# The second layer's row blocks run last to first, under one nested test, in a fused attention and two-MoE kernel

## The chip, the cores and the metric

One NeuronCore of a Trainium2 chip runs the whole program. The metric is the device time of one execution in microseconds; the times of the kernel before are 552.27, 552.94 and 557.62 us, median 552.94 us.

## What is computed

Chunked attention (2 x 8 heads, 768 tokens, head size 64, with 8 memory tokens) gives 1536 rows of 512. Two mixture-of-experts layers with 8 experts follow, each token going to its best expert. The reference, cut to the expert work of the second layer:

```python
expert_idx = np.argmax(logits, axis=1)          # logits = x @ w_gate
for i in range(N):                              # N = 1536, capacity = 384
    e = expert_idx[i]
    if counts[e] < capacity:
        disp[e, counts[e]] = x[i]; pos[i] = counts[e]; counts[e] += 1; keep[i] = True
h = np.maximum(np.einsum('ecd,edf->ecf', disp, w1), 0.0)   # D = 512, F = 1024
y = np.einsum('ecf,efd->ecd', h, w2)
out[i] = gate_w[i] * y[expert_idx[i], pos[i]]              # for kept tokens
```

## The kernel before, in words

The program is attention (to about 85 us), the routing of layer 0, eight experts of layer 0, the routing of layer 1 (about 313 to 329 us), and eight experts of layer 1. An order written out by hand holds on every engine: each engine runs its instructions in the order in which the code issues them.

A matmul in full precision is made of three: each fp32 operand is split into a rounded high part and a low remainder, and high x high, high x low and low x high are added up in one PSUM bank. So every weight half (w1 or w2 of one expert, 2 MB) is cut into 8 pieces; a piece costs a cast on ACT (L756, `whi`) and a subtraction on DVE or POOL (L757, `wlo`). The raw halves come by SP's DMAs into a ring of three slots, so a slot is loaded again only when all its pieces were cast and subtracted.

One expert of layer 1 (`layer_run`, layer 1) goes through these steps:

- `gather(e + 1)` and `scatter(e - 1)` are issued on POOL (indirect DMAs of the rows that go to the expert, and of its results).
- `first(e)`: h = relu(x w1) in eight products of 12 matmuls (L818 to L820), each in the next of four PSUM banks; their width is 224, 320 or 384 columns, chosen by up to two tests on the expert's number of tokens (`by_width`, the branches carry L775). ACT and DVE take each product into `hx` (L834, L835) and, between them, split the pieces of w2.
- `columns(e + 1)`: 12 transposes (L803) turn the next expert's rows into columns, into two of the four banks and one further; ACT (L807) and DVE (L808) copy them out.
- `second_rows(e)`: y = h w2, in blocks of 128 tokens. A block is 24 matmuls (L878 to L880) into one bank. Block 0 always runs; blocks 1 and 2 each stand under a `tc.If` on the token count (L885), so an expert runs one, two or three blocks. Between the blocks, the pieces of the next expert's w1 are split (3, 3 and 2 of them), and `rows` (L894) scales a finished block's bank into `yr` on ACT. The last expert already takes its blocks as 2, 1, 0, and scatters each as soon as it is scaled.

A `tc.If` on PE is: two register operations and a compare-and-branch, the body, a branch over the other arm, and in the other arm a wait on PE's own semaphore and a raise of it by what the body would have raised, so that waits of other engines count the same on both ways. The profile shows that wait as an EVENT_SEMAPHORE of PE's sequencer (PEq, L885).

Layer 0 uses `second_columns` in place of `second_rows` and is not touched.

Of the kernel before, what the change touches and what calls it, by code (L numbers as in the profile page):

```python
# [32 lines left out]
def kernel(  # L33
# [15 lines left out]
    nc = tc.nc  # L49
    B, _, _, D, _ = q.shape  # L50
    H, S = 2 * q.shape[1], SEQ
    N, DM = out.shape
    E, _, F = w1a.shape
    P = 128
# [6 lines left out]
    KF = F // P  # L61
# [3 lines left out]
    NA = CAP // P  # L65
    NAF = N // P
    XW = DM + E
    STEP = 32
# [14 lines left out]
    hx = [wpool.tile([P, KF, CAP], F32, name=f"hx{z}") for z in range(2)]  # L83
# [111 lines left out]
    def fr(ap):  # L195
        return ap.bitcast(F32R)
# [549 lines left out]
    def pieces(i, j, pool=(), done=0):  # L746

        if i < 2 * E:
            for n in range(PIECES):
                yield parts(i, j, n), nc.gpsimd if n in pool else nc.vector, n >= done  # L750

    def split(p):
        if p is not None:
            (w, h, l), eng, hi = p
            if hi:
                nc.scalar.copy(fr(h), w)  # L756
            eng.tensor_tensor(fr(l), w, h, op=ALU.subtract)  # L757

    def weights():
        v = [("p (c f) -> p c f", dict(c=KD)), ("p (c d) -> p c d", dict(c=KF))]  # L760
        return [(whi[j].rearrange(v[j][0], **v[j][1]), wlo[j].rearrange(v[j][0], **v[j][1])) for j in range(2)]
# [3 lines left out]
    def next_bank():  # L765
        return mm[next(turn_of) % 4]
# [13 lines left out]
    def layer_run(layer, src, r):  # L780
# [3 lines left out]
        ns = {}  # L784
# [77 lines left out]
        def second_rows(e, prep):  # L862

            w2h, w2l = weights()[1]
            yr = yrs[e % 2]
            pvs = {}

            order = list(range(NA)) if e < E - 1 else list(range(NA))[::-1]
            for n, a in enumerate(order):
                sl = slice(a * P, (a + 1) * P)  # L870
                ps = next_bank()
                pvs[a] = ps

                def emit():
                    for f in range(KF):
                        hh, hl = hx[0][:, f, sl], hx[1][:, f, sl]
                        wh, wl = w2h[:, f, :], w2l[:, f, :]
                        nc.tensor.matmul(ps, fr(hh), fr(wh), start=(f == 0), stop=False)  # L878
                        nc.tensor.matmul(ps, fr(hh), fr(wl), start=False, stop=False)  # L879
                        nc.tensor.matmul(ps, fr(hl), fr(wh), start=False, stop=(f == KF - 1))  # L880

                if a == 0:
                    emit()
                else:
                    with tc.If(ns[e] > a * P // STEP):  # L885
                        emit()
                for _ in range((3, 3, 2)[n]):
                    split(next(prep, None))
                if n > 0:
                    rows(e, order[n - 1], pvs)  # L890
            rows(e, order[-1], pvs)

        def rows(e, a, pvs):
            nc.scalar.activation(yrs[e % 2][:, a, 0:DM], pvs[a], AF.Copy, scale=sgate[:, e * NA + a:e * NA + a + 1])  # L894
            if e == E - 1:
                scatter(e, (a,))
# [33 lines left out]
        def scatter(e, blocks=range(NA)):  # L930
            for a in blocks:
                i_ = nc.gpsimd.indirect_dma_start(  # L932
                    dst, bass.IndirectOffsetOnAxis(ap=idx[:, e * NA + a:e * NA + a + 1], axis=0),
                    yrs[e % 2][:, a, 0:sw], None, bounds_check=N - 1, oob_is_err=False)
                scat.append(i_)
                if len(scat) > 1:
                    tc.declare_no_dep(i_.ins, group=f"scat{layer}", reason="slots hold distinct tokens")
                tc.add_to_no_dep_group(f"scat{layer}", i_.ins)
# [10 lines left out]
        for e in range(E):  # L949
# [11 lines left out]
            prep = pieces(i, 1, (3, 5, 7), EARLY[layer] if e == 0 else 0)  # L961
# [25 lines left out]
            prep = pieces(i + 1, 0, (2, 5))  # L987
            if layer == 0:
                second_columns(e, prep)
            else:  # L990
                second_rows(e, prep)
# [103 lines left out]
```

## Time and profile before

| what | value |
|---|---|
| median of three runs | 552.94 us |
| the profiled execution, device time | 552.76 us |
| its span in the trace | 550.9 us |
| PE busy | 504.0 us, 91% of the span |
| ACT busy | 307.0 us, 56% |
| DVE busy | 293.8 us, 53% |
| POOL busy | 240.0 us, 44% |
| DMA, mean | 182 GB/s |
| TensorE clock granted, mean | 0.964 |

A timeline row gives the start, the length, the engine, the line, the operation, its tiles and shapes, how many were merged, and in brackets the idle time of the engine just before it with what released it. A matmul's length is not its step: matmuls overlap in the array, and 24 of them with 512 columns start 0.23 us apart though each lasts 0.39 us. PEld is the weight load ahead of a matmul. Times in the trace count from the span's start.

### The profile page before, as it was taken

What the parts mean: (1) busy time and instruction counts of PE and PEld (TensorE: products, weight loads), DVE (VectorE), ACT (ScalarE), POOL (GpSimd) and SP (SyncE); (2) the same over time, 40 slices, a digit from 0 to 9 for tenths busy, and PEclk for the clock granted to TensorE, in tenths of its full rate; (3) what the DMA queues carried; (4) which work ended last, traced back from release to release, by engine and by line L of the source; (5) the groups of instructions that cost most, each with busy time, mean ns of one, the idle gap of its engine ahead of it and who ended that gap; (6) DMA issues with size and microseconds to landing.
All of it is one profiled execution on the core that took longest, in us unless ns stands there. A gap on an engine that the chain in (4) does not pass through costs nothing. (4 is left out here: it accounts for less than half of the span.)

```text
span 550.9 us, 11567 instructions
## 1 busy us (share of the span) xinstructions
PE 504.0 (91%) x3970; PEld 460.4 (84%) x3971; DVE 293.8 (53%) x735; ACT 307.0 (56%) x654; POOL 240.0 (44%) x242
## 2 busy tenths in 40 slices
PE   8899988899999999899999469899999998899991
PEld 5688856899999999899999439788889897798980
DVE  4576766634335255554436288874736284757320
ACT  6576774355445365655556374865646375655430
POOL 3042528253332445444353266665534446564230
PEclk9899988899999999999999878999999999989996
DMA  8899955742482265756465518867454637450000
GB/s 260 245 326 318 262 209 154 264 147 106 157 275 80 96 240 178 248 180 208 156 203 161 182 38 312 272 235 241 175 193 153 215 117 265 155 185 21 27 6 21
DMA packets 47574, 100.35 MB, mean 182 GB/s; under 512 B 11364, under 2 KB 12900, under 8 KB 47472
## 3 DMA queue, kind: packets, MB, share of 16 engines
q1 hardware_dynamic: 40000, 86.19, 46.7%
q0 software_dynamic: 7440, 12.71, 7.1%
q8 instruction: 74, 1.21, 0.9%
q14 instruction: 28, 0.23, 0.1%
q10 hardware_dynamic: 32, 0.02, 0.0%
HBM read 92.53 MB, written 18.22 MB: 201 GB/s over the span
## 5 line engine op out<-in xcount | busy, mean ns | idle before, releaser
L757 DVE TENSOR_TENSOR wlo<-raw,whi 128x512 fp32r<-128x512 f32 x159 | 129.5, 834 | 93.4 <-ACT whi L756 89.0
L757 POOL TENSOR_TENSOR wlo<-raw,whi 128x512 fp32r<-128x512 f32 x73 | 100.8, 1386 | 158.6 <-ACT whi L756 155.2
L818 PE MATMUL mm<-xs,whi 128*128 128x224 f32 (+2 forms) x480 | 144.2, 300 | 10.9 <-ACT whi L756 3.4
L820 PE MATMUL mm<-xs,wlo 128*128 128x224 f32 (+2 forms) x480 | 142.4, 297 | 1.9 <-issue 1.9
L819 PE MATMUL mm<-xs,whi 128*128 128x224 f32 (+2 forms) x480 | 142.3, 297 | 1.0 <-issue 1.0
L756 ACT CAST whi<-raw 128x512 fp32r<-128x512 f32 x218 | 128.1, 624 | 0.0
L818 PEld LDWEIGHTS mm<-xs,whi 128*128 128x128 f32 x480 | 94.0, 196 | 15.0 <-issue 6.7
L835 DVE SCALAR_TENSOR_TENSOR hx<-mm,hx 128x384 fp32r<-128x384 f32 x120 | 66.8, 557 | 72.9 <-ACT hx L834 66.2
L834 ACT ACTIVATE hx<-mm 128x384 fp32r<-128x384 f32 x120 | 59.3, 494 | 79.9 <-PE mm L820 76.1
L820 PEld LDWEIGHTS mm<-xs,wlo 128*128 128x128 f32 x480 | 94.0, 196 | 2.3 <-issue 2.3
L819 PEld LDWEIGHTS mm<-xs,whi 128*128 128x128 f32 x480 | 94.2, 196 | 1.3 <-issue 1.2
L818 PE MATMUL mm<-hx,whi 128*128 128x224 f32 (+2 forms) x224 | 67.2, 300 | 0.1
L820 PE MATMUL mm<-hx,wlo 128*128 128x224 f32 (+2 forms) x224 | 66.6, 297 | 0.0
L819 PE MATMUL mm<-hx,whi 128*128 128x224 f32 (+2 forms) x224 | 66.5, 297 | 0.0
L793 POOL DMA_INDIRECT xrow<-x_dram,idx x48 | 56.8, 1182 | 15.4 <-issue 10.5
L878 PE MATMUL mm<-whi,hx 128*128 128x512 f32 x128 | 51.2, 400 | 0.6 <-ACT hx L834 0.6
L880 PE MATMUL mm<-whi,hx 128*128 128x512 f32 x128 | 50.5, 394 | 0.0
L879 PE MATMUL mm<-wlo,hx 128*128 128x512 f32 x128 | 50.5, 394 | 0.0
L894 ACT ACTIVATE yr<-mm,sgate 128x512 f32<-128x512 f32 x24 | 16.0, 688 | 51.7 <-PE mm L880 51.7
L818 PEld LDWEIGHTS mm<-hx,whi 128*128 128x128 f32 x224 | 42.6, 190 | 0.3 <-issue 0.3
L819 PEld LDWEIGHTS mm<-hx,whi 128*128 128x128 f32 x224 | 42.6, 190 | 0.0
L820 PEld LDWEIGHTS mm<-hx,wlo 128*128 128x128 f32 x224 | 42.6, 190 | 0.0
(175 smaller groups left out, 656.2 us busy)
## 6 DMA issues: line engine op xcount, KB each, us to landing
raw<-in_moe_w_dram SPq DMA_DIRECT2D x128, 512.0 KB
v<-in_v_dram SPq DMA_DIRECT2D x24, 195.0 KB
kw<-in_k_dram SPq DMA_DIRECT2D x6, 576.0 KB
x_dram<-xr SPq DMA_DIRECT2D x12, 256.0 KB
out_dram<-zero SPq DMA_DIRECT2D x12, 256.0 KB
qt<-in_q_dram SPq DMA_DIRECT2D x6, 384.0 KB
kw<-in_k_dram SPq DMA_DIRECT2D x6, 192.0 KB
qt<-in_q_dram SPq DMA_DIRECT2D x6, 128.0 KB
```

The costliest lines, as they stand in the source:

```text
L756: nc.scalar.copy(fr(h), w)
L757: eng.tensor_tensor(fr(l), w, h, op=ALU.subtract)
L793: nc.gpsimd.indirect_dma_start(xrow[e % 2][:, a, 0:src.shape[1]], None, src, bass.IndirectOffsetOnAxis(ap=idx[:, e * NA + a:e * NA + a + 1 ...
L818: nc.tensor.matmul(ps[:, 0:L], fr(wh[:, k, cols]), xh, start=(k == 0), stop=False)
L819: nc.tensor.matmul(ps[:, 0:L], fr(wh[:, k, cols]), xl, start=False, stop=False)
L820: nc.tensor.matmul(ps[:, 0:L], fr(wl[:, k, cols]), xh, start=False, stop=(k == nk - 1))
L834: nc.scalar.activation(fr(hx[0][:, g, :]), hs[g], AF.Relu)
L835: nc.vector.scalar_tensor_tensor(fr(hx[1][:, g, :]), hs.pop(g), 0.0, hx[0][:, g, :], op0=ALU.max, op1=ALU.subtract)
L878: nc.tensor.matmul(ps, fr(hh), fr(wh), start=(f == 0), stop=False)
L879: nc.tensor.matmul(ps, fr(hh), fr(wl), start=False, stop=False)
L880: nc.tensor.matmul(ps, fr(hl), fr(wh), start=False, stop=(f == KF - 1))
L894: nc.scalar.activation(yrs[e % 2][:, a, 0:DM], pvs[a], AF.Copy, scale=sgate[:, e * NA + a:e * NA + a + 1])
```

## The change

In layer 1 every expert takes its blocks from the last to the first. The test for block 2 stands inside the body of the test for block 1, so an expert with one block takes one skip, an expert with two blocks one skip (the inner), and an expert with three none. Both tests come ahead of all blocks; block 0 runs last with nothing after it. The banks are given out as 2, 1, 0. The splitting of all 8 pieces of the next w1 is issued behind the blocks' matmuls and ahead of the three `rows`, which also go 2, 1, 0. The last expert's `rows` and scatters, which stood between its blocks, now stand behind all three.

```diff
-            pvs = {}
-
-            order = list(range(NA)) if e < E - 1 else list(range(NA))[::-1]
-            for n, a in enumerate(order):
+            pvs = {a: next_bank() for a in range(NA)[::-1]}
+
+            def block(a):
                 sl = slice(a * P, (a + 1) * P)
-                ps = next_bank()
-                pvs[a] = ps
-                def emit():
-                    for f in range(KF):
...
-                if a == 0:
-                    emit()
-                else:
-                    with tc.If(ns[e] > a * P // STEP):
-                        emit()
-                for _ in range((3, 3, 2)[n]):
-                    split(next(prep, None))
-                if n > 0:
-                    rows(e, order[n - 1], pvs)
-            rows(e, order[-1], pvs)
+                for f in range(KF):
...
+            def blocks(a):
+                with tc.If(ns[e] > a * P // STEP):
+                    if a + 1 < NA:
+                        blocks(a + 1)
+                    block(a)
+
+            blocks(1)
+            block(0)
+            for p in prep:
+                split(p)
+            for a in range(NA)[::-1]:
+                rows(e, a, pvs)
```

On PE, before, the end of the second expert's blocks and the start of the third expert's first product (`whi_65`, `wlo_66` are the split w1, `whi_1500`, `wlo_1501` the split w2, `mm_*` the four banks):

```order
L879 MATMUL mm_1494<-wlo_1501,hx_69 128x512
L880 MATMUL mm_1494<-whi_1500,hx_70 128x512
L885 UNCONDITIONAL_BRANCH
L885 UNCONDITIONAL_BRANCH [waits PE_49]
L775 REGISTER_ALU x2
L775 COMPARE_AND_BRANCH
L775 REGISTER_ALU x2
L775 COMPARE_AND_BRANCH
L818 MATMUL mm_1491<-xs_67,whi_65 128x384 [waits DVE_49,Activation_49]
```

The same place after the change:

```order
L874 MATMUL mm_1494<-whi_1500,hx_69 128x512 [waits Activation_49]
L875 MATMUL mm_1494<-wlo_1501,hx_69 128x512
L876 MATMUL mm_1494<-whi_1500,hx_70 128x512
L775 REGISTER_ALU x2
L775 COMPARE_AND_BRANCH
L775 REGISTER_ALU x2
L775 COMPARE_AND_BRANCH
L818 MATMUL mm_1491<-xs_67,whi_65 128x384 [waits DVE_49,Activation_49]
```

The wait on PE's own semaphore is gone from between the blocks and the next first product. Ahead of the blocks, after the change, stand the transposes and both tests:

```order
L803 MATMUL tp<-ident,xrow_1496 128x128 [waits DMASW5_49]
L803 MATMUL tp<-ident,xrow_1496 128x128 x3
L880 REGISTER_ALU x2
L880 COMPARE_AND_BRANCH
L880 REGISTER_ALU x2
L880 COMPARE_AND_BRANCH
```

and the arm that skips block 2 stands between block 2's end and block 1's first matmul:

```order
L875 MATMUL mm_1492<-wlo_1501,hx_69 128x512
L876 MATMUL mm_1492<-whi_1500,hx_70 128x512 [waits DVE_49]
L880 UNCONDITIONAL_BRANCH
L880 UNCONDITIONAL_BRANCH [waits PE_49]
L874 MATMUL mm_1493<-whi_1500,hx_69 128x512 [waits DVE_49,Activation_49]
L875 MATMUL mm_1493<-wlo_1501,hx_69 128x512
```

The wait has moved there: in an expert with two blocks it now follows the transposes. On ACT, before, at the same expert (`raw_0_8951` is the raw w1, `yr_1507` the results):

```order
L756 CAST whi_65<-raw_0_8951 128x4x128 [waits Pool_49]
L885 UNCONDITIONAL_BRANCH x2
L775 UNCONDITIONAL_BRANCH
L894 ACTIVATE yr_1507<-mm_1492,sgate_8353 128x512 [waits DMASW7_49,DMASW5_49,PE_49]
L756 CAST whi_65<-raw_0_8951 128x4x128 [waits Activation_49]
L775 UNCONDITIONAL_BRANCH
L756 CAST whi_65<-raw_0_8951 128x4x128 [waits Activation_49]
L894 ACTIVATE yr_1507<-mm_1493,sgate_8353 128x512 [waits DMASW0_49,DMASW6_49,DVE_49,PE_49]
L894 ACTIVATE yr_1507<-mm_1494,sgate_8353 128x512 [waits DMASW7_49,DVE_49,PE_49]
```

and after:

```order
L756 CAST whi_65<-raw_0_8951 128x4x128 [waits Pool_49]
L756 CAST whi_65<-raw_0_8951 128x4x128 [waits Activation_49] x2
L893 ACTIVATE yr_1507<-mm_1492,sgate_8353 128x512 [waits DMASW7_49,DVE_49,PE_49]
L893 ACTIVATE yr_1507<-mm_1493,sgate_8353 128x512 [waits DMASW0_49,DMASW6_49,DVE_49,PE_49]
L775 UNCONDITIONAL_BRANCH x3
L893 ACTIVATE yr_1507<-mm_1494,sgate_8353 128x512 [waits DMASW5_49,DVE_49,PE_49]
```

The last two casts no longer stand behind the first `rows`, and all three `rows` follow the casts.

## Rows read from the trace of the kernel before

**Rows 1.** Page, part 1: busy us (share of the span) x instructions, TensorE.

```profile
PE 504.0 (91%) x3970; PEld 460.4 (84%) x3971; DVE 293.8 (53%) x735; ACT 307.0 (56%) x654; POOL 240.0 (44%) x242
```

**Rows 2.** Waits of PE, 330 to 551 us: us in total, times, longest.

```profile
PE mm L818 <- ACT whi L756: 3.4, 2, 1.9
PE mm L818 <- issue: 2.5, 3, 1.3
PE mm L818 <- PEq L885: 1.7, 2, 1.0
```

**Rows 3.** Timeline of PE, from the blocks into the next expert's first product.

```profile
351.56 0.34 PE L818 MATMUL mm<-xs,whi 128*128 128x224 f32 x1 [1.49 <-ACT whi L756]
...
375.81 0.40 PE L880 MATMUL mm<-whi,hx 128*128 128x512 f32 x1
376.98 0.34 PE L818 MATMUL mm<-xs,whi 128*128 128x224 f32 x1 [0.77 <-PEq L885]
...
402.29 0.41 PE L818 MATMUL mm<-xs,whi 128*128 128x384 f32 x1 [0.96 <-PEq L885]
...
436.82 0.39 PE L880 MATMUL mm<-whi,hx 128*128 128x512 f32 x1
437.06 0.26 PE L818 MATMUL mm<-xs,whi 128*128 128x224 f32 x1
...
461.71 0.34 PE L818 MATMUL mm<-xs,whi 128*128 128x224 f32 x1 [1.32 <-issue]
...
482.58 0.38 PE L818 MATMUL mm<-xs,whi 128*128 128x320 f32 x1 [1.89 <-ACT whi L756]
```

**Rows 4.** Instructions of L885, then of L775: duration ns min/median/max, first and last start.

```profile
L885 PEldq COMPARE_BRANCH  x24: 68/175/344, 345.9 to 529.3; - x24
L885 PEldq EVENT_SEMAPHORE  x8: 51/51/51, 350.1 to 527.2; - x8
...
L775 PEldq COMPARE_BRANCH  x252: 67/208/3830, 88.9 to 523.9; - x126
```

**Rows 5.** Timelines of PE and DVE, from the transposes or first products into the blocks.

```profile
344.25 0.48 PE L878 MATMUL mm<-whi,hx 128*128 128x512 f32 x1
...
344.30 1.28 DVE L808 TENSOR_TENSOR xs<-mm,xs 128x512 fp32r<-128x512 f32 x2
...
389.59 0.60 PE L803 MATMUL tp<-ident,xrow 128*128 128x128 f32 x4
389.94 0.48 PE L878 MATMUL mm<-whi,hx 128*128 128x512 f32 x1
...
526.90 0.27 PE L820 MATMUL mm<-xs,wlo 128*128 128x224 f32 x1
527.80 0.47 PE L878 MATMUL mm<-whi,hx 128*128 128x512 f32 x1 [0.63 <-ACT hx L834]
```

**Rows 6.** Windows of 2 us: length, busy us of each engine, granted clock, DMA share, GB/s.

```profile
482.00:484.00 2.00, 1.42 (x10) 1.45 (x11) 1.25 (x2) 2.00 (x4) 1.69 (x2) 0.99 0.46 121
484.00:486.00 2.00, 2.00 (x9) 2.00 (x9) 1.18 (x2) 1.12 (x3) 1.41 (x2) 0.50 0.45 129
486.00:488.00 2.00, 2.00 (x12) 2.00 (x11) 0.74 (x2) 0.04 (x1) 1.68 (x2) 0.65 1.10 386
```

**Rows 7.** Timeline of ACT, the first expert's block and behind it.

```profile
345.09 3.24 ACT L756 CAST whi<-raw 128x512 fp32r<-128x512 f32 x6
350.10 0.69 ACT L894 ACTIVATE yr<-mm,sgate 128x512 f32<-128x512 f32 x1 [1.77 <-PE mm L880]
350.69 1.13 ACT L756 CAST whi<-raw 128x512 fp32r<-128x512 f32 x2
351.71 1.27 ACT L894 ACTIVATE yr<-mm,sgate 128x512 f32<-128x512 f32 x2
```

**Rows 8.** Timeline of PE, inside two experts' first products.

```profile
360.81 0.37 PE L818 MATMUL mm<-xs,whi 128*128 128x224 f32 x1 [0.98 <-DVE hx L835]
...
468.18 0.37 PE L818 MATMUL mm<-xs,whi 128*128 128x224 f32 x1 [0.88 <-issue]
```

More of the change, by code (lines that the diff above doesn't have):

```diff
@@ L865, in second_rows @@
             yr = yrs[e % 2]
-            pvs = {}
-            order = list(range(NA)) if e < E - 1 else list(range(NA))[::-1]
-            for n, a in enumerate(order):
+            pvs = {a: next_bank() for a in range(NA)[::-1]}
+            def block(a):
                 sl = slice(a * P, (a + 1) * P)
-                ps = next_bank()
-                pvs[a] = ps
-                def emit():
-                    for f in range(KF):
[L876 to L880, printed above, removed]
-                if a == 0:
-                    emit()
-                else:
-                    with tc.If(ns[e] > a * P // STEP):
-                        emit()
-                for _ in range((3, 3, 2)[n]):
-                    split(next(prep, None))
-                if n > 0:
-                    rows(e, order[n - 1], pvs)
-            rows(e, order[-1], pvs)
+                for f in range(KF):
+                    hh, hl = hx[0][:, f, sl], hx[1][:, f, sl]
+                    wh, wl = w2h[:, f, :], w2l[:, f, :]
+                    nc.tensor.matmul(pvs[a], fr(hh), fr(wh), start=(f == 0), stop=False)
+                    nc.tensor.matmul(pvs[a], fr(hh), fr(wl), start=False, stop=False)
+                    nc.tensor.matmul(pvs[a], fr(hl), fr(wh), start=False, stop=(f == KF - 1))
+            def blocks(a):
[9 more added lines that the diff above has]
+                rows(e, a, pvs)
         def rows(e, a, pvs):
```

## The prediction

> **What bounds the kernel now.** The page's first part comes first: PE is busy 504.0 of 550.9 us, every other engine under 60% [rows 1]. Time can only be won where PE stands idle or runs slowly. The second view is the list of PE's waits over the second layer's experts: nearly all of its idle time there is charged to L818, the first matmul of a first product, under three names, ACT, "issue" and PE's own sequencer [rows 2]. The third view, PE's timeline at those places, shows that most of this is one place: the step from an expert's last block to the next expert's first product. There are seven such steps. Five show idle times of 1.49, 0.77, 0.96, 1.32 and 1.89 us, 6.43 us together; two show none, as at 436.82 to 437.06 us, where the next product starts 0.24 us after the last block matmul [rows 3]. The two without idle time are those of the experts with three blocks. The 1.49 and 1.89 belong to the experts with one block.
>
> So the cause I read is not the name that the view gives. In a skipped `tc.If` PE's sequencer waits on PE's own semaphore, that is until the matmuls issued so far have ended. The trace has eight such waits [rows 4]: one in each of the three two-block experts among the first seven, two in each of the two one-block experts, and one in the last expert. Behind the wait come the width tests of the next product, and they now run with PE empty. Without a skip the sequencer runs ahead, and the same tests cost nothing (437.06). The two steps that are charged to ACT are the ones with two skips in a row, so I take ACT's cast as a bystander that ended nearby.
>
> The fourth view is the granted clock in windows. Behind the longest of these gaps (1.89 us before 482.58) the clock is 0.50 from 484 to 486 us and 0.65 from 486 to 488 us, the lower of the two levels (1.2 against 2.4 GHz) for most of that time [rows 6]. PE was busy the whole time, so 2 x (0.01 + 0.50 + 0.35) = 1.7 us of work were lost there.
>
> **The change part by part.** No matmul, cast, activation or DMA is added or removed; all are reordered.
>
> *Blocks to next product.* Block 0 stands last, with no test behind it, so all seven steps become like 436.82 to 437.06. Each of the five gains its idle time plus the overlap of neighbouring matmuls, 0.40 - 0.24 = 0.16 us: 6.43 + 5 x 0.16 = 7.2 us.
>
> *Transposes to first block.* The drain moves here, since the inner or outer skip now follows the transposes. Before, the block's first matmul starts under the last transposes: they end at 389.59 + 0.60 = 390.19, the block starts at 389.94 [rows 5]. With the drain it starts after 390.19 plus the time from the wait to a matmul. No row shows a drain with no test behind it. From below it is the wait instruction, 0.05 us [rows 4]; from above it is the 0.63 us at 527.80, which holds one drain and one further test [rows 5]. I take 0.30, about half, since the tests now stand ahead of the drain, where PE still has the first product's matmuls and the transposes to work through. That makes 390.49 against 389.94, 0.55 us for each of three two-block experts (0.30 to 0.88).
>
> The Trainium skill ("Advanced Engine Details and Errata", Control Flow Timing) puts a compare-and-branch at about 108 ns; rows 4 show 68 to 344 ns, median 175, for these. Taking only the page's 0.11 us out of the 0.63 would leave 0.52 in place of 0.30, and the total gain below would be 0.9 us smaller; the measured branches decide against it.
>
> *One-block experts.* Here block 0 is the first to run, and its bank is now the one that `columns` filled first, so it also waits for DVE's first copy (L808). Two copies take 1.28 us from 344.30 [rows 5], so the first ends near 344.97; with 0.09 us to the matmul block 0 starts at 345.06 in place of 344.25, 0.8 us. The other one-block expert repeats the pattern. So 1.6 us for the two (0.55 to 1.2 each). The bank of a two-block expert's first block was last read by DVE at the end of the first products, just under the transposes; the drain covers it.
>
> *Last expert.* Its order was 2, 1, 0 already; only a test moves ahead of the drain, 0.63 becomes 0.30: 0.3 us won (0 to 0.6). Its `rows` 2 and 1 (0.69 us each [rows 7]) and their scatters now stand behind the last block's matmuls in the code, but on ACT and POOL they wait only for their own blocks, and block 0 runs for 24 x 0.23 = 5.6 us over them. The chain at the end, block 0, its `rows`, its scatter, stays.
>
> *Casts and rows.* All eight casts now run at 3.24 / 6 = 0.54 us each [rows 7], 4.3 us, inside the first 5.6 us block. Their cost is nothing as long as a block covers them; without it the last two would hold the next products by 1.13 us, but those want pieces 6 and 7 only some 8 us later. `rows` 0 is now the last, one activation of 0.69 us behind the end of the blocks instead of two (1.27 us [rows 7]). Its bank is wanted by the fourth next product, three products of about 1.35 us later: 4 us of room. The scatters on POOL now wait for `rows` 0 and end about 1 us later; behind them on POOL stand w2 subtractions whose casts come later still. SP's next load waits for the last DVE subtraction, and DVE is not sped up, so the loads hardly move.
>
> *The clock.* With the 1.89 us gap gone, the largest idle time near 480 us is about 0.6 us. Gaps of 1.49 and 1.32 us in this trace were not followed by the low level, so I take the 1.7 us as won.
>
> *Sum.* -7.2 + 3 x 0.55 + 1.6 - 0.3 = -4.3 us from the drains, -1.7 us from the clock, together -6.0 us against the profiled execution's 552.76 us (0.2 us under the median): 546.8 us, 1.1% less.
>
> **The rivals.**
>
> *A. The clock falls anyway*, at this place or another, since the program's idle times shift. For it: one gap that was followed by it and two that were not are few cases. Against it: every gap gets shorter. 552.8 - 4.3 = 548.5 us.
>
> *B. The gap only moves.* The drain and two tests run with PE empty ahead of the blocks, 0.77 us and more as at 376.98, and the block's start under the transposes is lost too; or ACT was the true cause of the two large gaps. For it: the wait instruction is still there, once in each such expert. Against it: the tests stand ahead of it. 552 to 553 us, no change.
>
> *C. Slower: a skip has to fetch code.* L775's branches took up to 3.83 us [rows 4], and at 468.18 PE stood 0.88 us with nothing else to wait for [rows 8]. If the branches ahead of the blocks did that, it would fall on a drained PE: 6 skips at 2.5 us is 15 us, less the 6.0, 562 us. It eats the gain from 1.0 us a skip, and is slower by 1% from 1.9 us. Against it: L885's 24 branches never took over 0.344 us, and the skipped code is as long as before. The Trainium skill ("Runtime: NRT & Kernel Launch", Instruction fetch mechanics) states that a taken branch out of the loaded code pages must wait for a DMA to bring the target; by that rule the outer skip over two blocks is the one at risk, and no row of L885 here shows it.
>
> *D. Two stalls inside the first products*, 0.88 us at 468.18 and 0.98 at 360.81 [rows 8], go or double with the new phase: plus or minus 1.8 us on any case.
>
> **How the numbers follow.** Forecast 0.63, A 0.20, B 0.11, C 0.06. The ends of the sum are 7.2 - 0.9 - 1.1 + 0.6 = 5.8 and 7.2 - 2.6 - 2.4 = 2.2 us for the drains; with the clock and half of D the forecast reaches 544.8, and A with a poor drain 550.5. These are the range; it leaves out B and C. A measurement here can tell about 1%, 5.5 us, from no change: the line is at 547.3. Three quarters of the forecast lie below it, 0.47; a quarter of it, A and B lie within 1%, 0.48; C and a bad D are 0.05.
>
> **What would show it.** Right: L818 behind the blocks starts about 0.24 us after the last block matmul in all seven steps; the block's first matmul shows idle times of 0.3 to 0.6 us in five experts; no low clock between 335 and 540 us; the waits of L818 on ACT's cast are gone. Wrong: idle time at the blocks' start of 0.8 us and more, a low clock near 480 us, a branch of the nested tests over 1 us, or a wait of PE for a bank that `rows` holds.

## The result and the profile after

The changed kernel takes 545.33 us (median of four runs, 540.26 to 547.93) against 552.89 us for before; the ratio is 0.9847, with a 95% interval of 0.9803 to 0.989, so it is faster by 1.1 to 2.0%. The profiled execution of after took 547.93 us, its span is 546.1 us. The prediction was 546.8 us, with 0.47 on faster by over 1% and 0.48 on within 1%. Executions more than 1.5% above the fastest of their kernel count as slow and are left out of the medians and ratios here (four of twelve of casts only, one each of the changed kernel's second set and of else matmul).

What the two traced executions of after differ by lies mostly ahead of the changed part. So in this document I also use one stretch of each trace: from the end of the first second-layer expert's transposes (the last L803 of that group) to the end of the span. Before, those transposes end at 344.49 us, and the stretch is 550.9 - 344.49 = 206.4 us. After, it is 546.1 - 346.51 = 199.6 us: 6.8 us less, while the unchanged part ahead of it happened to be 2.0 us longer.

The waits of PE in that stretch after the change (engine, line, waited for: us in total, times, longest), to be held against [rows 2]:

```profile
PE mm L818 <- issue: 1.3, 2, 0.7
PE mm L874 <- DVE xs L808: 1.1, 2, 0.5
PE mm L874 <- ACT xs L807: 0.6, 2, 0.3
PE mm L874 <- DVE hx L835: 0.4, 1, 0.4
PE mm L874 <- PEq L880: 0.3, 1, 0.3
```

L818's waits for ACT's cast and for PE's own sequencer are gone. What is left of L818 is 1.3 us "issue". The first block matmul, L874, has new waits of 0.3 to 0.5 us at six places.

PE's timeline at the first expert's block and behind it, a two-block expert's blocks and the last expert (start, length, engine, line, operation, tiles, shapes, idle time before it with its releaser):

```profile
345.91 0.60 PE L803 MATMUL tp<-ident,xrow 128*128 128x128 f32 x4
347.05 0.50 PE L874 MATMUL mm<-whi,hx 128*128 128x512 f32 x1 [0.54 <-DVE xs L808]
...
352.51 0.39 PE L876 MATMUL mm<-whi,hx 128*128 128x512 f32 x1
352.74 0.27 PE L818 MATMUL mm<-xs,whi 128*128 128x224 f32 x1
...
377.24 0.40 PE L876 MATMUL mm<-whi,hx 128*128 128x512 f32 x1
377.48 0.27 PE L818 MATMUL mm<-xs,whi 128*128 128x224 f32 x1
...
390.28 0.60 PE L803 MATMUL tp<-ident,xrow 128*128 128x128 f32 x4
391.18 0.47 PE L874 MATMUL mm<-whi,hx 128*128 128x512 f32 x1 [0.30 <-ACT xs L807]
...
479.38 0.39 PE L876 MATMUL mm<-whi,hx 128*128 128x512 f32 x1
479.61 0.31 PE L818 MATMUL mm<-xs,whi 128*128 128x320 f32 x1
...
522.91 0.47 PE L874 MATMUL mm<-whi,hx 128*128 128x512 f32 x1 [0.30 <-PEq L880]
```

The next product now starts 0.23 us behind the last block matmul, also at 479.61, where before PE stood for 1.89 us [rows 3]. The block starts 0.30 us behind the end of the transposes (390.88 to 391.18) in a two-block expert (0.43 us in one of the three), and 0.54 us in a one-block expert, where DVE's first copy is waited for.

L880 after the change, to be held against L885 in [rows 4]:

```profile
L880 PEldq COMPARE_BRANCH  x22: 68/176/363, 344.9 to 524.4; - x22
L880 PEldq EVENT_SEMAPHORE  x6: 51/51/51, 346.6 to 522.7; - x6
```

Six drains instead of eight, and no branch of the nested tests over 0.363 us. The clock, in windows of 2 us over the place where it fell before (length, busy us of PE, PEld, DVE, ACT, POOL, granted clock, DMA share, GB/s), against [rows 6]:

```profile
478.00:480.00 2.00, 2.00 (x11) 1.69 (x10) 2.00 (x2) 1.64 (x4) 1.85 (x2) 1.00 1.00 406
480.00:482.00 2.00, 2.00 (x16) 2.00 (x15) 1.56 (x3) 1.44 (x4) 1.60 (x2) 1.00 0.34 69
482.00:484.00 2.00, 2.00 (x15) 2.00 (x14) 1.29 (x3) 1.18 (x4) 1.48 (x2) 1.00 0.98 301
```

It stays at 2.4 GHz there. ACT at the first expert, against [rows 7]:

```profile
347.11 4.28 ACT L756 CAST whi<-raw 128x512 fp32r<-128x512 f32 x8
351.28 1.27 ACT L893 ACTIVATE yr<-mm,sgate 128x512 f32<-128x512 f32 x2
352.94 0.69 ACT L893 ACTIVATE yr<-mm,sgate 128x512 f32<-128x512 f32 x1 [0.39 <-PE mm L875]
```

All eight casts end 1.5 us ahead of the block, the two empty `rows` follow, and only the last `rows` waits for the block.

### The profile page after: what moved, and what is told of

It is laid out like the page before. It is cut to its first block, busy times and chain, and to the rows that moved or that the text cites. A ratio compares the mean times of both kernels' runs of the same rounds, so it can differ in the third digit from the quotient of the medians.

```text
span 546.1 us, 11554 instructions
## 1 busy us (share of the span) xinstructions
PE 504.7 (92%) x3970; PEld 460.6 (84%) x3971; DVE 292.9 (54%) x735; ACT 306.1 (56%) x654; POOL 236.3 (43%) x242
## 5 line engine op out<-in xcount | busy, mean ns | idle before, releaser
L818 PE MATMUL mm<-xs,whi 128*128 128x224 f32 (+2 forms) x480 | 143.4, 299 | 5.2 <-DVE hx L835 2.9
L820 PE MATMUL mm<-xs,wlo 128*128 128x224 f32 (+2 forms) x480 | 141.8, 295 | 0.7 <-issue 0.7
L818 PEld LDWEIGHTS mm<-xs,whi 128*128 128x128 f32 x480 | 93.5, 195 | 7.8 <-DVE hx L835 4.6
L820 PEld LDWEIGHTS mm<-xs,wlo 128*128 128x128 f32 x480 | 93.5, 195 | 0.8 <-issue 0.8
L818 PE MATMUL mm<-hx,whi 128*128 128x224 f32 (+2 forms) x224 | 67.3, 300 | 0.5 <-issue 0.5
L820 PE MATMUL mm<-hx,wlo 128*128 128x224 f32 (+2 forms) x224 | 66.6, 297 | 0.0
L793 POOL DMA_INDIRECT xrow<-x_dram,idx x48 | 53.1, 1107 | 15.5 <-issue 10.7
L874 PE MATMUL mm<-whi,hx 128*128 128x512 f32 x128 | 51.2, 400 | 2.4 <-DVE xs L808 1.1
L818 PEld LDWEIGHTS mm<-hx,whi 128*128 128x128 f32 x224 | 42.6, 190 | 0.8 <-issue 0.8
L820 PEld LDWEIGHTS mm<-hx,wlo 128*128 128x128 f32 x224 | 42.6, 190 | 0.0
```

What stands on the lines that cost most here:

```text
L793: nc.gpsimd.indirect_dma_start(xrow[e % 2][:, a, 0:src.shape[1]], None, src, bass.IndirectOffsetOnAxis(ap=idx[:, e * NA + a:e * NA + a + 1 ...
L818: nc.tensor.matmul(ps[:, 0:L], fr(wh[:, k, cols]), xh, start=(k == 0), stop=False)
L820: nc.tensor.matmul(ps[:, 0:L], fr(wl[:, k, cols]), xh, start=False, stop=(k == nk - 1))
L874: nc.tensor.matmul(pvs[a], fr(hh), fr(wh), start=(f == 0), stop=False)
```

## The experiments

Two theories stood against each other. **Drain theory**: what costs time is a skipped test's wait on PE's own semaphore, because the width tests and the next product then start on an empty PE; the change moves this wait to a place where less follows it. **Cast theory**, the rival: the views name ACT's cast as what ended the largest waits, so the casts' new place carries the gain. The stretch defined above, in us, for all traces. Each ratio is to executions of before that were taken beside the kernel; their medians lie between 552.4 and 554.4 us, so kernels are better compared by ratio than by time:

| kernel | stretch | time, median | ratio to before (95%) |
|---|---|---|---|
| before, two traces | 206.4, 206.9 | 552.89 | |
| after, two traces | 199.6, 199.1 | 545.33 and 545.04 | 0.985 (0.980 to 0.989), 0.987 (0.981 to 0.993) |
| casts only | 206.7 | 551.03 | 0.994 (0.990 to 0.998) |
| order only | 199.0 | 546.68 | 0.989 (0.984 to 0.993) |
| flat reverse | 199.6 | 545.49 | 0.988 (0.983 to 0.992) |
| nested forward | 204.3 | 550.34 | 0.997 (0.993 to 1.001) |
| drain back | 209.5 | 556.52 | 1.004 (1.001 to 1.007) |
| else matmul | 196.7 | 545.17 | 0.986 (0.980 to 0.992) |
| own banks | 210.4 | 558.17 | 1.010 (1.004 to 1.017) |
| own banks 2 | 198.3 | 546.62 | 0.986 (0.982 to 0.990) |
| else and own banks | 214.2 | 559.98 | 1.013 (1.007 to 1.018) |
| else and own banks 2 | 198.6 | 543.65 | 0.982 (0.979 to 0.986) |

**The changed kernel again.**

> The changed kernel again, for a second trace and more times. Drain theory: the part from the first matmul of the second layer's first expert to the span's end takes 215.0 us again (550.9 - 329.35 = 221.6 us before, 546.1 - 331.15 = 215.0 us in the first trace of after), within 0.5 us, and what the times of one kernel differ by lies ahead of it, in the part that is unchanged. Rival: the second layer's part itself differs between executions by several us, and the gain of a single trace is chance.

The stretch is 540.7 - 341.60 = 199.1 us, and the idle times ahead of the blocks are 0.55, 0.30, 0.30, 0.30, 0.53 and 0.30 us. Its execution took 542.5 us, 5.4 us less than the first profiled one; 4.9 us of that lie ahead of the stretch (transposes end at 341.60 instead of 346.51). The gain of the changed part repeats, and the spread comes from the unchanged one.

**Before again.**

> The kernel before once more, for a second trace. Drain theory: 206.4 us from the end of the first expert's transposes to the span's end, as in the first trace, within 1 us, with the same five idle times at the same steps (1.5, 0.8, 1.0, 1.3, 1.9 us); what its time differs by lies ahead. Rival: the five idle times are chance and differ by more than 0.3 us each.

The stretch is 548.4 - 341.47 = 206.9 us. The idle times at the five steps are 1.40, 0.77, 0.96, 1.33 and 1.84 us. Two things differ. Inside the second expert's first products PE stands 2.51 us where the first trace had 0.98 [rows 8], and behind the 1.84 us gap the clock does not fall. PE's timeline and the windows:

```profile
359.24 0.37 PE L818 MATMUL mm<-xs,whi 128*128 128x224 f32 x1 [2.51 <-DVE wlo L757]
...
481.02 0.39 PE L818 MATMUL mm<-xs,whi 128*128 128x320 f32 x1 [1.84 <-ACT whi L756]
```

```profile
482.00:484.00 2.00, 2.00 (x15) 2.00 (x15) 1.12 (x2) 1.55 (x4) 1.70 (x2) 1.00 0.73 168
484.00:486.00 2.00, 2.00 (x16) 2.00 (x15) 1.38 (x4) 1.05 (x3) 1.39 (x3) 1.00 0.99 329
```

So the five idle times belong to the kernel, and the low clock near 484 us only to some of its executions.

**Casts only**, the order and tests of before with the casts ahead of the rows:

```diff
-                for _ in range((3, 3, 2)[n]):
-                    split(next(prep, None))
-                if n > 0:
-                    rows(e, order[n - 1], pvs)
-            rows(e, order[-1], pvs)
+            for p in prep:
+                split(p)
+            for a in order:
+                rows(e, a, pvs)
```

> The order and the tests of before, but all eight casts ahead of the three rows. Drain theory: nothing changes, about 552.9 us, and the five idle times at the step from the blocks to the next product stay (6.4 us together), the two of 1.5 and 1.9 us among them, with the low clock near 484 us. Rival (ACT's cast ends the two largest waits, as the view of waits names it): those two fall to under 1.2 us, and with the clock the time falls by 1 to 4 us, to 549 to 552 us.

By the time alone the rival is not out: the median is 551.03 us against 553.22 us for before, inside the rival's 549 to 552, and the ratio's interval of 0.990 to 0.998 means a gain of 0.2 to 1.0%. The one trace does not show this gain in the changed part: its stretch is 206.7 us. The idle time that the view of waits had put down to ACT's cast is the same, 1.89 us, and now carries DVE's name; the clock falls behind it again (0.70, then 0.50):

```profile
352.57 0.34 PE L818 MATMUL mm<-xs,whi 128*128 128x224 f32 x1 [1.49 <-DVE wlo L757]
...
483.86 0.38 PE L818 MATMUL mm<-xs,whi 128*128 128x320 f32 x1 [1.89 <-DVE wlo L757]
```

```profile
484.00:486.00 2.00, 2.00 (x11) 2.00 (x12) 0.69 (x1) 0.36 (x1) 1.70 (x2) 0.70 0.77 210
486.00:488.00 2.00, 2.00 (x10) 2.00 (x8) 0.84 (x2) 1.00 (x2) 1.39 (x3) 0.50 0.92 255
```

The cast theory falls by the gaps: with the casts early, both large ones stay (1.49 and 1.89 us), where the rival put them under 1.2. Where the small gain in the time lies is not shown.

**Order only**, after with the casts back at 6 and 2:

```diff
-            for p in prep:
-                split(p)
-            for a in range(NA)[::-1]:
+            for n, a in enumerate(range(NA)[::-1]):
+                for _ in range((6, 2, 0)[n]):
+                    split(next(prep, None))
                 rows(e, a, pvs)
```

> The order, the nested tests and the banks of after, but only six of the eight casts ahead of the first rows, the last two between the first and the second, as before had them. Drain theory: as after, about 545.3 us, the second layer's part 215 us. Rival (the casts' place carries a part of the gain): the first products wait for the late casts again, 1 to 3.4 us more, 546.5 to 549 us.

199.0 us, as after; no wait of L818 for a cast returns. PE's waits in the stretch:

```profile
PE mm L874 <- DVE xs L808: 1.1, 2, 0.5
PE mm L874 <- ACT xs L807: 0.9, 3, 0.3
PE mm L818 <- issue: 0.7, 2, 0.4
PE mm L874 <- PEq L880: 0.3, 1, 0.3
PE mm L820 <- issue: 0.2, 1, 0.2
```

(The expectation's "215 us" counts from the first product instead; the stretch says the same.) The time, 546.68 us, lies in the rival's range too, but cannot be told from after's; the stretch and the waits decide. The order of the blocks carries the gain, the place of the casts none that shows.

**Flat reverse**, the two tests in a row instead of nested:

```diff
-            def blocks(a):
-                with tc.If(ns[e] > a * P // STEP):
-                    if a + 1 < NA:
-                        blocks(a + 1)
-                    block(a)
-            blocks(1)
+            for a in (2, 1):
+                with tc.If(ns[e] > a * P // STEP):
+                    block(a)
             block(0)
```

> As after, but the two tests stand one behind the other and not nested, block 2's test and body first: a one-block expert drains twice, and a test stands between drain and matmul. Drain theory: 0.3 us more at each of six places (0.63 against 0.30 idle), the second layer's part 216.9 us, about 547 us. Rival (only the order counts, nesting is free): 215 us, as after.

The idle times ahead of the blocks did rise, to 0.67, 0.72, 0.63, 0.53, 0.77 and 0.63 us, 3.95 us together against 2.40 in the first trace of after: 1.55 us where 1.9 was expected. The stretch does not show it, 199.6 us: this trace has only 0.36 us of stalls inside the first products, where after had 1.3. So nesting saves most of what was expected at its place (in the last expert 0.30 against 0.63 us: one test behind the drain is 0.33 us), and that is too little to see in the time.

**Nested forward**, block 0 first, the nested tests behind it, casts as after; banks and `rows` go 0, 1, 2 too, also in the last expert:

```diff
-                    if a + 1 < NA:
-                        blocks(a + 1)
-                    block(a)
-            blocks(1)
-            block(0)
+                    block(a)
+                    if a + 1 < NA:
+                        blocks(a + 1)
+            block(0)
+            blocks(1)
```

> Block 0 first, then block 1 under its test and block 2 under a test nested in that, casts ahead of rows as in after: the drain stands again at the step to the next product, but a one-block expert has one drain and one test less. Drain theory: the idle times at the two-block experts' ends stay at 0.8 to 1.3 us, those at the one-block experts' ends fall from 1.5 and 1.9 to about 1.0 and 1.4 us: 205.5 us from the end of the first transposes against 206.4 for before, and 203.8 us if the clock no longer falls near 484 us. Rival (nesting and the casts carry the gain of after, not the place of the drain): about 200 us.

204.3 us, inside the expected 203.8 to 205.5, and 550.34 us. The gaps stand at the step to the next product again: 0.97 and 1.28 us for the one-block experts, 1.07, 1.29 and 1.55 us for the others, 0.2 to 0.3 us longer than in before, which nothing here explains. PE's timeline at the longest:

```profile
463.77 0.34 PE L818 MATMUL mm<-xs,whi 128*128 128x224 f32 x1 [1.55 <-ACT yr L893]
```

The clock fell behind none of the five. Nesting and early casts alone do not make the gain; where the wait stands does.

**Drain back**, after with only the wait put back behind block 0 (the condition never holds, so the body is left out and its skip remains):

```diff
             block(0)
+            with tc.If(ns[e] > CAP // STEP):
+                nc.tensor.matmul(pvs[2][:, 0:P], ...)
```

> As after, with one thing added: between block 0 and the next expert's first product stands the skip of a body that never runs, which leaves only its wait on PE's own semaphore, in all seven steps and behind the last expert. No other instruction is added. Drain theory: each step shows 0.8 to 1.3 us of idle time again, 0.94 to 1.5 us each with the lost overlap, 7.6 us in all: 206.7 to 207.2 us from the end of the first expert's transposes against 199.1 to 199.6 us for after, and about 553 us, the time of before. Rival (the wait is cheap and it was the tests, the late casts or ACT that held PE): under 3 us more.

This is the direct measurement. Every step has its gap, also those behind three-block experts, which had none before; PE's timeline at one of each:

```profile
380.56 0.34 PE L818 MATMUL mm<-xs,whi 128*128 128x224 f32 x1 [0.78 <-PEq L887]
...
441.13 0.34 PE L818 MATMUL mm<-xs,whi 128*128 128x224 f32 x1 [0.68 <-PEq L887]
```

and the instruction that was added, eight times 51 ns of work:

```profile
L887 PEldq EVENT_SEMAPHORE  x8: 51/51/51, 353.6 to 543.5; - x8
```

The seven gaps are 0.98, 0.78, 0.96, 0.68, 1.33, 1.27 and 0.81 us, 6.8 us, and 7.9 with the lost overlap of 0.16 each; 7.6 was expected. The stretch is 209.5 us, 10 us above after. The rest is 1.4 us behind the last expert, where all three `rows` now wait for the added wait, and stalls in the first products of 1.05 and 0.65 us, 0.4 to 0.8 us more than in after. The time is 556.52 us, 0.1 to 0.7% slower than before, where about the time of before was expected.

**Else matmul**, after with a short matmul per skipped block in an else arm:

```diff
+            def short(a):
+                nc.tensor.matmul(pvs[a][:, 0:P], fr(hx[0][:, 0, 0:P]), fr(w2h[:, 0, 0:P]), start=True, stop=True)
             def blocks(a):
-                with tc.If(ns[e] > a * P // STEP):
+                with tc.If(ns[e] > a * P // STEP) as more_rows:
...
+                with more_rows.Else():
+                    for c in range(a, NA)[::-1]:
+                        short(c)
```

> As after, but each skipped body has an else arm of one short matmul per skipped block (128 columns, into that block's bank, whose result no row of the output uses), so that this matmul raises PE's semaphore and no wait on PE's own semaphore is left. Drain theory: the 0.30 us of idle time ahead of the block in the two-block experts and the last go, about 0.5 us at each of four places; the one-block experts go on waiting for DVE's first copy, 0.5 us. From the end of the first expert's transposes to the span's end: 199.1 to 199.6 us for after, 197.0 to 197.7 us here. Rival (the jump itself empties PE, not the wait): idle times and 199 us stay.

The drain is gone and the block runs up to the transposes again; PE's timeline at a two-block and a one-block expert:

```profile
358.80 0.60 PE L803 MATMUL tp<-ident,xrow 128*128 128x128 f32 x4
359.15 0.31 PE L880 MATMUL mm<-whi,hx 128*128 128x128 f32 x1
359.36 0.47 PE L874 MATMUL mm<-whi,hx 128*128 128x512 f32 x1
```

```profile
341.31 0.50 PE L874 MATMUL mm<-whi,hx 128*128 128x512 f32 x1 [0.28 <-DVE xs L808]
```

The stretch is 196.7 us, 0.3 below the expected range and 2.4 to 2.9 under after. So it is the wait that empties PE, not the jump. In the time, 545.17 us, this does not show beside the spread of the unchanged part.

**Own banks**, after with `pvs = {a: tps[a] for a in range(NA)}`:

> As after, but the three blocks write to three PSUM banks of their own, which the second layer does not use otherwise. Bank theory (the one-block experts wait for DVE's first copy because block 0 takes the bank that the transposes filled first): idle time ahead of their block falls from 0.54 to 0.30 us, 0.5 us in all, 198.6 to 199.1 us from the end of the first transposes. Rival (that wait was only named, the drain takes as long): no change.

A miss: 558.17 us. PE stands 1.72 to 1.82 us ahead of the blocks of seven experts, the three-block ones too. The wait is named after ACT's cast; PE starts 0.15 us behind the end of DVE's copy of the third transposes (362.47 + 0.68 = 363.15). PE's timeline, then a row of DVE's:

```profile
360.88 0.60 PE L803 MATMUL tp<-ident,xrow 128*128 128x128 f32 x4
363.30 0.47 PE L874 MATMUL tp<-whi,hx 128*128 128x512 f32 x1 [1.82 <-ACT whi L756]
...
362.47 0.68 DVE L808 TENSOR_TENSOR xs<-tp,xs 128x512 fp32r<-128x512 f32 x1
```

The banks are slices of the PSUM tile `tp`, whose fourth slice takes the third transposes. A second version gives those a bank of the rotating four instead (`tps[3] if layer == 0 else next_bank()`):

> Banks of their own for the blocks, as in own_banks, but the third bank of the transposes now comes from the four rotating ones, so that blocks and transposes share no PSUM tile. Theory for the 1.8 us that own_banks showed ahead of every block: the block had to wait for the copies of a bank that belongs to the same PSUM tile. Then the idle times fall to 0.30 us in all skipping experts and to none in the three-block ones: 198.5 to 199.1 us from the end of the first transposes. Rival (those banks are slow to write, or the wait is for the rows of the expert before): 1.8 us stay, 210 us.

The 1.8 us are gone; the idle times are 0.15 us in five of the six skipping experts (0.26 in one) and none in the three-block ones, under the 0.30 expected; where the other 0.15 us of after comes from is not shown. The stretch is 198.3 us. It loses 1.3 us at the end, where the three `rows` of the last expert now run together behind the last block, 0.69 us for one becoming 1.84 us for three, since their banks belong to one tile; ACT's timeline of the last rows:

```profile
531.21 1.84 ACT L893 ACTIVATE yr<-tp,sgate 128x512 f32<-128x512 f32 x3 [11.05 <-PE tp L876]
```

With both banks versions the else arms were tried as well:

> Both: else arms of short matmuls and banks of their own. Drain and bank theory: no idle time of over 0.1 us between transposes and block in any expert, 196.4 to 197.2 us from the end of the first transposes, and a time some 2.5 us under that of after, about 543 us. Rival (the block then waits for the activations that end the first products): idle times of 0.2 to 0.5 us stay, named after ACT or DVE hx.

The 1.8 us wait stays, 559.98 us, as in own banks. Neither the theory nor the rival of that expectation had it: the rival looked for 0.2 to 0.5 us behind the activations. In seven experts with gaps of 1.81 to 1.83 us the clock fell behind two, at 391 and near 456 us; in own banks, with gaps of 1.72 to 1.82 us, behind none.

> The same banks with the else arms of short matmuls. If both theories hold, no idle time of over 0.1 us between transposes and block, 196.0 to 196.8 us from the end of the first transposes, some 3 us under after, about 543 us. Rival: the wait of 1.8 us as in else_own, 210 us.

543.65 us, ratio 0.982 (0.979 to 0.986), the lowest median of all, but its interval overlaps that of after. No drain is left. The stretch is 198.6 us and not 196.0 to 196.8: 1.3 us are the rows at the end as above, and this trace has four stalls in the second and third expert (0.42, 0.67, 0.35, 0.65 us) that no other trace has together. Whether they belong to the kernel one trace does not tell.

## Why the prediction was right, and where it was wrong

**What bounds the kernel: right.** That the waits named after ACT were the drain of a skipped test was the main reading. Casts only left those gaps as they were, else matmul took the wait out and the gap went, drain back put it in and all seven steps had theirs.

**Blocks to next product: right.** All seven steps start at 0.23 to 0.24 us. The 7.2 us were taken from the rows; drain back measures 7.9 us for seven steps.

**Transposes to first block: right in size.** 0.30 us of idle time was an estimate between 0.05 and 0.63; the row at 391.18 shows 0.30 (another two-block expert 0.43), and the second trace 0.30 in all three. The last expert counts as a sixth place beside the five that the signs named. For the one-block experts 0.8 us each was predicted: the block starts 0.54 us behind the transposes' end instead of 0.24 us ahead of it, 0.78. The reason given for it, DVE's first copy, holds too: with other banks the wait for DVE is gone. The last expert went from 0.63 to 0.30 as written. With the steps of the first trace the drains give -7.2 + 3.3 - 0.3 = -4.2 us; -4.3 was predicted.

**The clock: a size that belongs to some executions.** The low clock behind the 1.9 us gap cost what rows 6 show in the first trace of before and again in casts only, and was not there in the second trace of before behind 1.84 us. The sum counted it as won in every execution. On average over executions the term is smaller than 1.7 us; two traces of before do not say by how much. In both traces of after the clock stays at 2.4 GHz from 336 us to the end of the last block, close to the 335 to 540 us of the signs.

**Stalls inside the first products: the term that was left out of the sum.** They stood in the text as D, going either way. They went one way. The kernels with a drain at the step to the next product show 1.7 to 4.0 us of them, counting the waits of L818 in the stretch (first trace of before 0.98 + 0.27 + 0.88, second 2.51 + 0.27 + 0.95 + 0.28, casts only 1.13 + 1.26, nested forward 1.62 + 0.93, drain back 1.05 + 0.65). All others show 0.3 to 1.3 us (after 1.28 and 0.90, order only 0.74, flat reverse 0.36, else matmul 0.70, the four with own banks 0.31 to 1.07). So a drain ahead of the products goes with longer stalls in them, some 1.8 us more on average over these traces.

The traces also show where the long ones come from. Each stall of 0.8 us and more stands directly behind one branch of the width test: PE runs on for 1.95 us from the branch's start with the matmuls that it was already given, then stands until the branch ends. In before the branch ahead of 360.81 [rows 8] takes 2.88 us and PE stands 0.98 us; at the same place of after it takes 2.52 us (from 358.99), PE is busy to 360.94 and stands 0.62 us. The branch in before, then in after, and PE's timeline of after:

```profile
L775 PEldq COMPARE_BRANCH  x1: 2883/2883/2883, 357.9 to 357.9; - x1
L775 PEldq COMPARE_BRANCH  x1: 2517/2517/2517, 359.0 to 359.0; - x1
...
360.66 0.27 PE L820 MATMUL mm<-xs,wlo 128*128 128x224 f32 x1
361.56 0.37 PE L818 MATMUL mm<-xs,whi 128*128 128x224 f32 x1 [0.62 <-issue]
```

The 1.95 us are the same with the drain and without (1.48 us once, in drain back), so it is the branches that are longer: 2.5 to 4.4 us with the drain, 2.3 to 2.5 us in the other kernels where PE stood behind one at all. Why they are longer is not shown. And drain back, which adds the drain alone, shows 1.05 us behind this branch against 0.62 and 0.54 us in the two traces of after, so the drain may not account for all of the difference.

**The step that failed: D, put at nothing in the sum, and the chances that followed.** The text had D at plus or minus 1.8 us on any case, so the sum held none of it. It ended at 546.8 us, 0.5 us under the 1% line, and the chances put as much on one side of the line as on the other, with slightly more on no change. The measured gain is 1.5% (1.1 to 2.0) and 1.3% (0.7 to 1.9) in the two sets of runs. From the first trace of before to the first of after, the rows give 4.2 us for the drains and 1.7 us for the clock, as the sum had them, and 1.0 us for D (2.3 us of stalls became 1.3, the waits of L820 counted too): 6.9 us, against 6.8 us by the stretch. From the second trace of before they give 4.1, nothing for the clock and 2.9 us for D: 7.0 us, against 7.3. So D was 1.0 and 2.9 us, both times on the side of the gain. The rows held a hint: the stalls stood in the first products behind a drained step [rows 8], and none in the products behind the three-block experts, though there were none behind 402.29 and 482.58 either. With half of D counted as gain, 0.9 us, the sum would have been 6.9 us and the line clear. Two smaller things pushed the same way. The line itself, 1% as what a measurement can tell, was coarse: the interval measured is 0.4% to either side. And rival A, whose 0.20 went to no change, did not come: in the seven traces of kernels without an idle time of over 0.8 us the clock fell nowhere between 346 us and the end of the last block.

The range was right, with a slip in its lower end: 5.8 us for the drains, 1.7 for the clock and half of D's 1.8 give 544.4 us, not 544.8. The measured 545.33 us lies above both.

**Rivals B and C: out.** The gap does not move at full size (0.30 against 0.77), and no branch of the nested tests took over 0.363 us. The rule on instruction fetch (the Trainium skill, "Runtime: NRT & Kernel Launch", Instruction fetch mechanics) is that a taken branch out of the loaded pages waits for a DMA. No such wait shows at these skips; the long L775 branches may be cases of it, which no run here shows.

**Casts, rows, tail: right.** Order only and after cannot be told apart, and the chain at the end is what it was.

## What to carry to other kernels

A conditional whose skipped arm waits for its own engine costs little by its instructions (51 ns here) and much by what stands behind it: 0.7 to 1.6 us behind one skip when further tests and the next product follow, 0.15 to 0.43 us when only matmuls do, no idle time when the other arm holds a short real instruction instead of the wait. So put tests ahead of the long straight piece of work, nest them so that one skip serves for all, and end on the part that always runs.

When a profile names another engine as what ended a wait, look whether the same step without the conditional shows the wait; here the two three-block experts pointed to it before any run, and the runs bore it out. And where a cost stands behind the thing that is being removed and not elsewhere, do not count it as noise on both sides: give its going a larger chance than its doubling.

## What the runs showed of the hardware

PE's granted clock fell to the lower level (1.2 GHz) behind gaps of 1.8 to 1.9 us in some executions and places and not in others: behind 1.89 us in two traces, not behind 1.84 us in a third, behind two of seven gaps of 1.8 us in one kernel, and behind none of seven in another. A gap of that size makes the loss possible, it does not make it certain.

Work on different banks of one PSUM tile was ordered as if it touched the same data: 1.8 us ahead of each block in own banks, and 1.84 us of rows at the end instead of 0.69. With the transposes in another tile, and so in another bank, the wait ahead of the blocks was gone, while the blocks kept their banks.

A long branch on PE's sequencer cost only what went beyond 1.95 us, in all places but one: branches of the width test of up to 1.84 us left PE busy, one of 2.52 us stopped it for 0.62 us and one of 4.40 us for 2.51 us.
